# Key-value sums in 32-column strips, fewer transpose instructions for weights, and a re-ordered instruction list in a fused attention and MLP kernel

## The chip, the cores and the metric

The kernel runs on one core of a Trainium2 chip. The metric is device time in microseconds (us) from launch to end; lower is better. The engines are named as in the profile: PE (TensorE, matrix products; PEld are its weight loads), DVE (VectorE), ACT (ScalarE), POOL (GpSimd) and SP (the queue that issues most DMA transfers).

## The reference

`x` has 2048 tokens of 448 features. It is normalised once (`xn`), and two blocks read `xn`; the result is `x` plus both.

```python
x = A_x
xn = _layernorm(x, axis=-1)
return x + _A_ref(xn, ...) + _B_ref(xn, ...)

# A: 16 heads of 28 features
pq = einsum("bhsd,hdf->bhsf", q, w_phi);  pk = einsum("bhsd,hdf->bhsf", k, w_phi)
phi_q = concatenate([softmax(pq), softmax(-pq)]);  phi_k = concatenate([softmax(pk), softmax(-pk)])
kv  = einsum("bhsf,bhsd->bhfd", phi_k, v);   z = einsum("bhsf->bhf", phi_k)
num = einsum("bhqf,bhfd->bhqd", phi_q, kv);  den = einsum("bhqf,bhf->bhq", phi_q, z)
o = num / (den + 1e-6)                       # and o @ wo

# B
h = gelu(layernorm(xn) @ w1);  hs = (four column groups of h, shifted by 1, -1, 2, -2 tokens) @ w2
x1 = xn + hs;  result x1 + gelu(layernorm(x1) @ w3) @ w4
```

Here `q`, `k`, `v` are the three 448-column parts of `xn @ wqkv`.

## The kernel before

Tokens are cut into 16 tiles of 128 (`NT`). The 448 features lie as four chunks that overlap (`lap`), so that a product over 448 features is two streams of 64-row matmuls, one in the upper and one in the lower half of the array's rows, which are issued in turn and run side by side (`LO`, `HI`, `row_pairs`). The profile prints such matmuls as `64*128`, and those that use all rows as `128*128`.

`Recorder` writes every instruction into a list per engine and works out the semaphore waits from what each reads and writes; each engine then runs its list in order. So the order of the calls in the source is the order of each queue. For PE it also keeps the tile mode (rows in use): a write to a bank that was last written in another mode waits for that earlier matmul. All operations are issued from a few helper lines: L204 (matmul), L208 (PE transpose), L212 (ACT), L216 (DVE and POOL), L219 (DMA transpose), L222 (DMA).

Three parts run one after the other, with overlap.

1. The head and the chain (`chain`, a hand-written list). `spin` and `hold` (`HD`) are filler matmuls on constants. For each tile: statistics on DVE (`"m"`), root on ACT or POOL (`"q"`, `"r"`), scaling on DVE (`"a"`) or on POOL (`"p"`, which first issues a negation), then the transposition of the tile into `xnT`: by PE (`XT`: 8 transposes of 64 columns, `xn_T`, and a copy out of PSUM, `xn_out`) or by a DMA transpose on SP (`XD`, `xn_Td`). With `xnT` come the value projection (`ZV`: 7 matmuls of 448 columns), the w1 product (`ZW`, `ZH`, `ZR`), and `fold` (`FO`), which multiplies the query and the key weights by `w_phi` ahead of the tokens: the weights come transposed by DMA (`load_wT`) into `wT`, and `phi_blocks` multiplies `w_phi` by a block mask `mb`, which POOL builds from a memset and two selects, into `bd`. `rest_T` turns the last columns of `h` into `hRT`, and `h_shift` makes the shifted copies by DMA. `HF` are the halves of the first key pair (0), the first w2 pair (1) and the first query pair (2).
2. The middle, from the list under `play`: per pair of tiles the key product (`k0`, `k1`, exponentials on ACT), the query product (`q0`, `q1`), the w2 product (`w0`, `w1_`, with the sum `w2_out` on DVE), `kn` (reduction and reciprocal on DVE), `kx` (the product with the reciprocal on POOL), `lo`, `sc`, `A`, `G` (second layernorm and its transposition), and `K`, the key-value sums of one tile (`kv_tile`).
3. The end: `a`, `b` (w3 product and gelu), `N` (`num_tile`: numerators, division), `f` (w4 and wo products), `S` (stores).

`kv_tile` takes, for one tile, 16 matmuls of 59 columns: `phik` is the stationary operand and `vaug` (values, a column of ones, a column of zeros for each head) streams, over 64 tokens each, into banks 6 and 7. After the last tile `kv_copy` adds the two banks (two DVE operations), `kv_blocks` moves rows by four matmuls with `pick`, and two DVE and two ACT copies write `kvq`, which `num_tile` reads.

Of the kernel before, what the change touches and what calls it, by code (L numbers as in the profile page):

```python
# [224 lines left out]
def bass_parallel_sum__linear_kernel_hedgehog__mixer_s_mlp__prompt_kernel(  # L225
# [17 lines left out]
    with es:  # L243
# [55 lines left out]
        bd = view(g_r, D)  # L299
        wphi = view(g_r, NC * DH, at=1024).rearrange("p (c f) -> p c f", c=NC)  # L300
        kvq = new("kvq", 8 * 64).rearrange("p (b e) -> p b e", b=8)
        kvT = view(w1_r, 512)
        kvf = view(w1_r, 512, F32, at=1024)
        pick = view(w1_r, 2 * 128, at=3072).rearrange("p (s c) -> p s c", s=2)
        ident = new("ident", 128)
        maskb = new("maskb", CR)
# [73 lines left out]
        R.dma(wphi[0:CR, :, :], A_w_phi.rearrange("(c q) e f -> (q e) c f", q=4))  # L380
# [17 lines left out]
        def load_w4(eng="SP"):  # L398
# [21 lines left out]
        mb = maskb[0:CR, :].rearrange("p (h e) -> p h e", h=4)  # L420
        R.ew(pool, "memset", maskb[0:CR, :], 1.0)
        R.op(pool, lambda e: e.affine_select(mb, mb, pattern=[[-DH, 4], [0, DH]], compare_op=ALU.is_ge,
                                             fill=0.0, base=0, channel_multiplier=1), [maskb[0:CR, :]], [maskb[0:CR, :]])
        R.op(pool, lambda e: e.affine_select(mb, mb, pattern=[[DH, 4], [0, DH]], compare_op=ALU.is_ge,
                                             fill=0.0, base=DH - 1, channel_multiplier=-1),
             [maskb[0:CR, :]], [maskb[0:CR, :]])

        def phi_blocks():
            R.ew(dve, "tensor_tensor", bd[0:CR, :].rearrange("p (c h f) -> p c h f", c=NC, h=4),
                 wphi[0:CR, :, :].unsqueeze(2).to_broadcast([CR, NC, 4, DH]),  # L430
                 mb.unsqueeze(1).to_broadcast([CR, NC, 4, DH]), op=ALU.mult)

        def late_3():
            pad = phik.rearrange("p t g e -> p (t g) e")[:, :, DH:HP]
            R.op(pool, lambda e: e.memset(pad, 0.0), [pad], [xn[:, NT - 2, :]])
            R.ew(pool, "memset", kvq[:, :, :], 0.0)
            R.ew(pool, "memset", eq[:, 4:8, :, :, DH:HP].rearrange("p t s h e -> p (t s h) e"), 0.0)

        def kv_ones():
            for h in range(4):  # L440
# [53 lines left out]
        def fold(t, m, b, n):  # L494
            def side(k, hi):
                r, c0, c1 = (slice(64, CR), 2 * DH, CR) if hi else (slice(0, 64), 0, 3 * DH)
                return [(banks[b + k][:, CR * c + c0:CR * c + c1],
                         wT[r, t, c, START[m + k]:START[m + k] + 128], bd[r, CR * c + c0:CR * c + c1], n == 0 and c == 0)
                        for c in range(NC)]
# [62 lines left out]
        def chain(jobs, lag, even):  # L562
            at, upper, seen = [0, 0], deque(), {}
            odd, left = False, sum(j[0] == "zip" for j in jobs)
# [37 lines left out]
            for kind, make, then, *mid in jobs:  # L602
# [12 lines left out]
                else:  # L615
                    for n, item in enumerate(make(LO, (0, 1, 3) if odd else (0, 1, 2, 3))):
# [6 lines left out]
                    left -= 1  # L623
                    odd = not odd and left > even
# [478 lines left out]
```

## Time and profile before

| | |
|---|---|
| median of 3 runs | 171.56 us (170.79 to 171.65) |
| profiled execution: span from its first to its last instruction | 169.2 us (the page has no other time for it) |
| median less that span | 2.4 us |
| PE busy | 165.9 us (98%), 2359 matmuls recorded |
| DVE, ACT, POOL busy | 109.6, 82.1, 92.2 us |
| matmuls of the key-value sums | 256 of 59 columns |
| PE transposes of xn tiles | 112 of 64 columns |
| DMA transposes of query and key weights | 8 |

The profile gives, for groups of instructions, the busy time and the mean length of one. Matmuls are pipelined and their ends are modelled, so what a matmul takes from PE is read from one start to the next. A timeline row has the start in us, the busy time in us, the engine, the line, the operation and its tiles, and the number of instructions merged.

### The profile page before, as it was taken

Reading aid. Unit: us, or ns where it says so; the run is one execution under the profiler, and the core shown is the slowest. Engines: PE = TensorE matmul, PEld = TensorE weight load, DVE = VectorE, ACT = ScalarE, POOL = GpSimd, SP = SyncE. Lnnn points to the kernel's source line nnn. Section 1 sums busy time; section 2 is a strip of 40 time slices with the busy share of each in tenths; the row PEclk is TensorE's granted clock in tenths of the full one; section 3 lists DMA queues with packets and bytes.
Section 4 is the critical chain, followed back from the end, with each engine's and each line's share of the span. In section 5 each row is a group of like instructions: output and inputs, shape, how many; then the busy total and the mean of one; then the engine's idle time right before and its main releaser. Section 6 shows DMA issues by size and latency. Waiting matters only on the chain.

```text
span 169.2 us, 5423 instructions
## 1 busy us (share of the span) xinstructions
PE 165.9 (98%) x2359; PEld 99.3 (59%) x2359; DVE 109.6 (65%) x248; ACT 82.1 (49%) x110; POOL 92.2 (54%) x124
## 2 busy tenths in 40 slices
PE   8999999999999999999999999999999999999994
PEld 7776778667786555554554555555545555444453
DVE  3998866159999899929685896718617586220031
ACT  3599975797998878646242422024204041144000
POOL 5288980005999999951792264396730845404040
PEclk9999999999999999999999999999999999999999
DMA  5995579999599985671076664434554422310031
GB/s 162 364 197 103 98 135 293 164 330 149 99 141 183 278 97 149 86 134 27 7 118 127 95 135 55 84 73 42 135 68 93 59 61 62 83 60 4 0 109 54
DMA packets 50567, 19.93 MB, mean 118 GB/s; under 512 B 41712, under 2 KB 49840, under 8 KB 50544
## 3 DMA queue, kind: packets, MB, share of 16 engines
q1 hardware_dynamic: 49424, 18.71, 57.1%
q10 hardware_dynamic: 1120, 0.89, 1.6%
q8 instruction: 18, 0.29, 0.8%
q14 instruction: 5, 0.04, 0.1%
HBM read 7.14 MB, written 1.84 MB: 53 GB/s over the span
## 4 chain that ended last, share of the span: by engine, by line
PE 95%; DMA 1%; DVE 1%; issue 0%; DVEq 0%
PE banks L204 94%; DMA xtok<-in_A_x_dram 1%; PE banks L208 1%; DVE st L216 1%; DVE mv L216 0%; DVE xn L216 0%; DVE vaug L216 0%; DVEq L166 0%
## 5 line engine op out<-in xcount | busy, mean ns | idle before, releaser
L212 ACT ACTIVATE phik<-banks 128x1024 bf16<-128x1024 f32 (+1 forms) x44 | 42.2, 987 | 60.7 <-PE banks L204 60.5
L216 DVE TENSOR_TENSOR vaug<-banks,vaug 128x464 f32<-128x464 f32 (+3 forms) x65 | 32.8, 513 | 26.1 <-PE banks L204 24.5
L204 PE MATMUL banks<-gT,w 64*128 64x512 bf16 x392 | 48.2, 376 | 0.0
L204 PE MATMUL banks<-w,phik 64*128 64x448 bf16 (+3 forms) x434 | 45.2, 343 | 0.0
L216 POOL TENSOR_TENSOR xnT<-vaug 128x196 bf16<-128x196 f32 (+1 forms) x32 | 18.1, 587 | 29.6 <-DVE vaug L216 29.6
L204 PEld LDWEIGHTS banks<-w,phik 64*128 64x128 bf16 (+1 forms) x434 | 22.3, 94 | 20.1 <-issue 0.4
L204 PE MATMUL banks<-wv,xnT 64*128 64x448 bf16 (+2 forms) x222 | 32.9, 346 | 0.0
L723 POOL TENSOR_TENSOR phik<-phik,rks 128x1792 bf16<-128x1792 bf16 x8 | 25.6, 3219 | 8.5 <-DVE rks L216 8.5
L204 PEld LDWEIGHTS banks<-gT,w 64*128 64x128 bf16 x392 | 17.9, 94 | 18.0 <-ACT phik L212 0.4
L216 POOL TENSOR_TENSOR vaug<-xn,xtok 128x448 f32<-128x448 bf16 x16 | 16.2, 1034 | 12.7 <-DVE vaug L216 12.7
L204 PEld LDWEIGHTS banks<-wv,xnT 64*128 64x128 bf16 (+1 forms) x222 | 14.0, 94 | 7.7 <-PE banks L204 0.3
L204 PE MATMUL banks<-xnT,w 64*128 64x512 bf16 (+1 forms) x105 | 16.6, 334 | 0.0
L204 PE MATMUL banks<-wpk,xnT 64*128 64x448 bf16 x112 | 16.6, 349 | 0.0
L216 DVE TENSOR_REDUCE ksum<-phik 128x64 f32<-128x1792 bf16 x8 | 16.0, 2000 | 0.0
L204 PE MATMUL banks<-wpq,xnT 64*128 64x448 bf16 x112 | 15.7, 349 | 0.0
L212 ACT ACTIVATE hi<-banks 128x896 bf16<-128x896 f32 x16 | 13.7, 923 | 2.0 <-PE banks L204 2.0
L204 PE MATMUL banks<-w,hT 64*128 64x448 bf16 x96 | 13.6, 349 | 0.0
L216 POOL TENSOR_TENSOR rs<-mv,mhalf 128x1 f32<-128x1 f32 (+1 forms) x13 | 9.4, 727 | 6.2 <-DVE mv L216 6.0
L216 DVE RECIPROCAL vaug<-banks 128x16 f32<-128x16 f32 x16 | 4.0, 250 | 12.6 <-PE banks L204 12.6
L216 DVE TENSOR_TENSOR xn<-banks,xn 128x512 bf16<-128x512 f32 (+1 forms) x16 | 8.9, 598 | 2.3 <-PE banks L204 2.3
L216 POOL TENSOR_SCALAR g_tok<-xn,rs 128x512 bf16<-128x512 bf16 x13 | 9.9, 774 | 0.2
L216 DVE BATCH_NORM_STATS2 st<-xtok 128x6 f32<-128x448 bf16 x16 | 9.6, 601 | 0.2 <-DMA xtok<-in_A_x_dram 0.2
(67 smaller groups left out, 172.7 us busy)
## 6 DMA issues: line engine op xcount, KB each, us to landing
w<-in_B_w_dram SPq DMA_DIRECT2D x2, 896.0 KB, 5.8
out_dram<-vaug SPq DMA_DIRECT2D x15, 112.0 KB, 1.8
w<-in_B_w_dram SPq DMA_DIRECT2D x1, 1568.0 KB, 8.6
xtok<-in_A_x_dram SPq DMA_DIRECT2D x2, 448.0 KB, 6.3
wv<-in_A_wo_dram SPq DMA_DIRECT2D x2, 224.0 KB, 3.3
xtok<-in_A_x_dram SPq DMA_DIRECT2D x3, 112.0 KB, 3.6
xtok<-in_A_x_dram ACTq DMA_DIRECT2D x3, 112.0 KB, 4.2
w<-in_B_w_dram SPq DMA_DIRECT2D x1, 336.0 KB, 4.1
```

The costliest lines, as they stand in the source:

```text
L204: self.op("PE", lambda e: e.matmul(out, lhsT, rhs, start=start, stop=stop, skip_group_check=True), [out], [lhsT, rhs], tile=self._tile(lhsT))
L208: self.op("PE", lambda e: e.transpose(out, in_, ident), [out], [in_, ident], tile=self._tile(in_))
L212: self.op("ACT", lambda e: e.activation(out, in_, func, **kw), [out], [in_] + aps)
L216: self.op(eng, lambda e: getattr(e, name)(out, *args, **kw), [out], aps)
L723: R.op(pool, lambda e: e.tensor_tensor(ph, ph, wide, op=ALU.mult), [ph], [ph, wide, *after])
```

## The change

- `kv_tile` swaps the operands: `vaug` of one head (30 columns) is stationary, `phik` (64 columns: both softmax signs of the head) streams, over all 128 tokens. Four heads go to four strips of 32 output rows in bank 6. There are still 16 matmuls a tile, now of 64 columns. In the list the calls of `K` stand in three groups on PE: 6, 5 and 5 tiles.
- `kv_turn` (a DVE transpose of 128 x 256 from PSUM) and `kv_blocks` (one DVE product with a mask `pick` of two columns) replace the two-bank add, the four matmuls and the copies.
- `load_wT` transposes two chunks of 128 columns in one DMA: four instructions instead of eight, placed at other points of the chain. The chunks are 128 columns wide instead of 112, so the mask covers 128 rows by 672 columns (112 by 112 before), `phi_blocks` has two operations, and `fold` takes three or four heads at a time: 48 matmuls of 84 and 8 of 112 columns instead of 32 of 84 and 32 of 56.
- Tiles 14, 13, 12 and 8 are transposed by DMA too (`XB`), besides 10 and 11. 80 PE transposes instead of 112.
- POOL scales 13 of the first-layernorm tiles (8 before), the first two among them; six tiles of the second layernorm are scaled on DVE (three before).
- The chain, the list under `play`, the banks and the split of each product between the two row halves (a string of 0 and 1) are new. The numerators (`num_tile`) stay as they are.

The core of the diff:

```diff
-        bd = view(g_r, D)
+        bd = view(g_r, NC * 6 * DH).rearrange("p (c h f) -> p c h f", c=NC, h=6)
+        mb = view(g_r, NC * 6 * DH, at=1600).rearrange("p (c h f) -> p c h f", c=NC, h=6)
...
-        def load_wT(t, cs):
-            for c in cs:
-                e0 = t * D + CR * c
-                R.dma_t(wT[:, t, c, 0:D], A_wqkv[:, e0:e0 + 128], after=[wv] if t and not c else [])
-        load_wT(1, (0, 1, 2, 3))
-        load_wT(0, (0,))
+        def load_wT(t, c, n=2):
+            R.dma_t(wT[:, t, c:c + n, 0:D], A_wqkv[:, t * D + 128 * c:t * D + 128 * (c + n)], after=[wv])
...
-        R.ew(pool, "memset", maskb[0:CR, :], 1.0)
+        R.ew(pool, "memset", mb[:, :, :, :], 1.0)
...
         def kv_tile(i):
-            def side(k, rows):
-                return [(banks[6 + k][:, 64 * n:64 * n + VP + DH + 1],
-                         phik[rows[0]:rows[1], i, 4 * n:4 * n + 4, :].rearrange("p g e -> p (g e)"),
-                         vaug[rows[0]:rows[1], i, 2 * VP * n:2 * VP * n + VP + DH + 1]) for n in range(8)]
-            row_pairs(side(0, LO), side(1, HI), i == 0)
+            for n in range(4):
+                for j in range(4):
+                    h = 8 * (j // 2) + 2 * n + j % 2
+                    R.mm(banks[6][HP * j:HP * j + VP, 64 * n:64 * n + 64], vaug[:, i, VP * h:VP * h + VP],
+                         phik[:, i, 2 * h:2 * h + 2, :].rearrange("p g e -> p (g e)"), i == 0 and n == 0, False)
...
-        def kv_copy():
-            n61 = [a.rearrange("p (n e) -> p n e", n=8)[:, :, 0:VP + DH + 1] for a in (banks[6], banks[7], kvf, kvT)]
-            R.ew(dve, "tensor_copy", n61[2], n61[0])
-            R.ew(dve, "tensor_tensor", n61[3], n61[1], n61[2], op=ALU.add)
+        def kv_turn():
+            R.ew(dve, "transpose", kvT[:, :], banks[6][:, 0:256])
...
+            R.ew(dve, "tensor_tensor", kvq[:, :, 0:2 * VP].rearrange("p b (h e) -> p b h e", h=2)[:, :, :, 0:DH + 1],
+                 kvT.rearrange("p (b e) -> p b e", e=HP)[:, :, 0:DH + 1].unsqueeze(2).to_broadcast([128, 8, 2, DH + 1]),
+                 pick.unsqueeze(1).unsqueeze(3).to_broadcast([128, 8, 2, DH + 1]), op=ALU.mult)
...
+        def XB(i):
+            return "both", ((), ()), ((xn_Td, i),)
...
-            L(("m", 0), ("q", 0, 1)), do(load_wT, 0, (1, 2, 3)), L(("m", 1), ("q", 1, 1), ("a", 0), ("a", 1)), HD(3, 3),
-            HD(6, 3), HD(3, 3), L(("m", 2)), XT(0, 0, 1, "ACT"), L(("q", 2, 1)), HD(6, 3), L(("m", 3), ("m", 4)),
-            XT(1, 2, 1, "ACT"), L(("p", 2), ("q", 3, 1), ("q", 4, 1), ("a", 3)), HD(6, 3), HD(6, 3), ZV(0, EV(0, "ACT", 1)),
...
-            do(h_shift, 1), do(kv_picks), HF(1, 1), do(rest_T, 1)], 400, 0)
+            L(("m", 0)), L(("q", 0, 1)), HD(4, 3), HD(4, 3), L(("p", 0)), HD(0, 3), L(("m", 1)), L(("m", 2)),
+            L(("q", 1, 1)), L(("m", 3)), L(("p", 1)), L(("q", 2, 1)), XT(0, 6, 1, "ACT"), XT(1, 1, 1, "ACT"),
+            L(("p", 2)), do(load_phi), L(("m", 4)), HD(5, 3), ZV(0, EV(0, "ACT", 1)), L(("q", 3, 1)), L(("r", 4, 1)),
...
+            inside(3, ZR(0, 5, (rest_out, 0, 5), (rest_T, 0)), XT(9, 1, 1, "2")), FO(0, 0, 0), XB(10),
+            ZV(9, EV(9, "ACT", 1)), do(load_w2), do(h_shift, 0), ZR(1, 4, (rest_out, 1, 4)), FO(0, 0, 1),
+            ZV(11, EV(11, "ACT", 1)), do(kv_ones), FO(0, 2, 0), ZW(2, 2, EW(2, 2, 1)), ZW(2, 1, EW(2, 1, 1)),
+            ZW(2, 0, EW(2, 0, 1)), do(rest_T, 1), FO(0, 2, 1), ZV(10, EV(10, "ACT", 1)), HF(0, 0), do(load_w4),
+            HF(1, 0), do(late_3), HF(2, 0), do(h_shift, 1), HF(0, 1), HF(1, 1), HF(2, 1), do(load_w3, 0)], 400,
+            "101100100101011100011010010101100")
```

More of the change, by code (lines that the diff above doesn't have):

```diff
@@ L495, in side @@
             def side(k, hi):
[L496 to L499, printed above, removed]
+                r = []
+                for c, (h0, h1) in enumerate(((2, 5), (2, 6), (3, 6)) if hi else ((0, 3), (0, 3), (1, 4), (1, 4))):
+                    p = slice(64 * hi, 64 * hi + 64)
+                    r.append((banks[b + k][:, DH * (4 * c + h0):DH * (4 * c + h1)],
+                              wT[p, t, c, START[m + k]:START[m + k] + 128],
+                              bd[p, c, h0:h1, :].rearrange("p h f -> p (h f)"), n == 0 and c == 0))
+                return r
             return side(n, 0), side(1 - n, 1)
@@ L560, in v_out, with chain @@
                 R.ew(dve, "tensor_copy", vd, vs)
-        def chain(jobs, lag, even):
+        def chain(jobs, lag, heavy):
             at, upper, seen = [0, 0], deque(), {}
-            odd, left = False, sum(j[0] == "zip" for j in jobs)
+            turns = iter(heavy)
             def where(item):
@@ L744, in kv_blocks @@
[L744 to L757 removed]
+                R.ew(dve, "memset", pick[HP * q:HP * q + HP, q % 2:q % 2 + 1], 1.0)
```

148 lines of the change are left out of this document (66 added, 82 removed).

## The prediction

> **What bounds the kernel now.** I read the busy shares of the page first, then the chain in order of time, then the busy time by stage, then PE's timeline around each edit.
>
> ```profile
> span 169.2 us, 5423 instructions
> PE 165.9 (98%) x2359; PEld 99.3 (59%) x2359; DVE 109.6 (65%) x248; ACT 82.1 (49%) x110; POOL 92.2 (54%) x124
> ```
> ```profile
> 5.33 0.40 PE banks L208 x8
> ...
> 13.24 0.14 PE banks L208 x8
> ...
> 16.56 0.35 PE banks L208 x24
> ...
> 24.82 142.05 PE banks L204 x1955
> 166.87 0.02 issue
> ```
> ```profile
> 34.00:80.00 46.00, 46.00 (x702) 28.77 (x700) 39.81 (x65) 36.64 (x43) 33.53 (x20) 1.00 0.81 152
> ```
>
> From 5.33 us to 166.87 us the chain is PE alone; its last piece, 142 us long, has no other releaser in it. Between 34 and 80 us, where the key-value sums lie, PE is busy for all 46.00 us, and DVE (39.81) has little room. So the time is a head of 5.3 us, the matmuls, and a tail of 2.3 us. An edit gains what it takes off PE and loses what it adds to the head or opens as a hole. Work taken off ACT or DVE gains nothing by itself.
>
> The sum is made on the span of the profiled execution, 169.2 us; the page gives no other time for it. The median of the runs, 171.56 us, is 2.4 us above that span (the runs 1.6 to 2.5), and I carry those 2.4 over. A measurement of this kernel can tell about 0.5% (0.86 us) from no change.
>
> **Key-value sums: what they cost now.** Per token tile, 16 matmuls of 59 columns, on two 64-row halves of the array at once.
>
> ```profile
> 73.77 1.67 PE L204 MATMUL banks<-gT,w 64*128 64x512 bf16 x14
> 75.27 0.62 PE L204 MATMUL banks<-vaug,phik 64*128 64x59 bf16 x32
> 75.73 1.67 PE L204 MATMUL banks<-gT,w 64*128 64x512 bf16 x14
> 77.39 0.39 PE L204 MATMUL banks<-w 64*128 64x232 bf16 x4
> 77.60 1.68 PE L204 MATMUL banks<-gT,w 64*128 64x512 bf16 x14
> ```
>
> A row's start to the next row's start is what a group takes from PE (the printed length holds the last one's pipeline too). Two token tiles take 75.73 - 75.27 = 0.46 us, 0.23 each, 14.4 ns a matmul; one half starts one every 28.8 ns. Sixteen tiles: 3.7 us.
>
> After, there are again 16 matmuls a tile, now 128 rows by 30 output columns with 64 columns streamed, in four column strips that all write bank 6. No row shows column strips. Bounds: if the four run at once, each strip at the pace of the 64-column transposes (24 in 0.35 us on two halves, 29.2 ns a half), 7.3 ns a matmul, 0.117 us a tile, 1.9 us in all: 1.8 less. If only two starts fit in that time, 14.4 ns: nothing gained. If they queue, 28.8 ns: 7.4 us, 3.7 more. I take the first: the two halves now start within the same slot and neither slows the other, and the strips write disjoint partitions as the halves use disjoint rows.
>
> **What the new shape adds.** The sums leave the 64-row mode. Before they lay in it between other 64-row matmuls; after they stand on PE in three groups (tiles 0, 9, 3, 2, 8, 1; then 10, 5, 4, 12, 7; then 15, 13, 6, 14, 11), so six changes of mode. The trace has one such change at full speed:
>
> ```profile
> 158.78 0.92 PE L204 MATMUL banks<-w,phik 64*128 64x448 bf16 x8
> 159.54 0.73 PE L204 MATMUL banks<-wv,xnT 64*128 64x448 bf16 x6
> 160.20 2.82 PE L204 MATMUL banks<-w,phik 128*128 128x448 bf16 x14
> ```
>
> Eight take 159.54 - 158.78 = 0.76 us, 95 ns each; six more would end at 160.11, and the 128-row one starts at 160.20: 0.09 us. Six cost 0.54 us (bounds 0, if it drains under other work, and 1.1, twice that). Key-value net: -1.8 + 0.5 = -1.3 us.
>
> [...]
>
> **The turn of the sums.** Four pick matmuls go (77.60 - 77.39 = 0.21 us), and PE's wait before them: the 14 ahead start at 75.73 and, like those at 73.77 (1.50 us to the next row), would end at 77.23; 0.16 us until 77.39. The DVE transpose and multiply that replace two copies, an add and casts stand before the first numerators; 28 matmuls of 107 ns (3.0 us) lie between on PE as cover. Without it their length would be a hole. I bound that by what they replace:
>
> ```profile
> 75.93 0.65 DVE L216 COPY w<-banks 128x472 f32<-128x472 f32 x1 [3.01 <-PE banks L204]
> ...
> 78.01 0.76 DVE L216 CAST kvq<-banks 32x232 bf16<-32x232 f32 x2
> ```
>
> From 75.93 to 78.77 is 2.8 us, less than the cover. Net -0.21 - 0.16 = -0.37 us.
>
> **xn tiles by DMA.** Tiles 14, 13, 12 and 8 join 11 and 10 on the DMA path: 32 transposes of 14.6 ns go, -0.47 us, and four DMA transposes are added on SP. Four for query/key weights (two chunks each) replace eight:
>
> ```profile
> 5.74 13.09 SPq L219 DMA_TRANSPOSE hi<-in_A_wqkv_dram  x8
> 18.88 2.26 SPq L222 DMA_DIRECT2D w<-in_B_w_dram  x3
> 21.18 2.58 SPq L219 DMA_TRANSPOSE xnT<-xn  x2
> 23.80 0.96 SPq L222 DMA_DIRECT2D w<-in_B_w_dram  x1
> 24.80 3.74 SPq L222 DMA_DIRECT2D hT<-hT  x6
> 28.59 1.31 SPq L219 DMA_TRANSPOSE hRT<-gT  x1
> ```
>
> One weight transpose holds SP 1.64 us, one xn tile 1.29. If a two-chunk one costs no more, SP is freed of 6.5 us and takes on 5.2; if twice, nothing is freed and 5.2 are added. What counts is the order: w2, the six shifts and hRT now stand behind tile 10's transpose, which waits for POOL to scale tile 10. The w2 matmuls that need them began here:
>
> ```profile
> 33.36 0.35 PE L204 MATMUL banks<-w,hT 64*128 64x448 bf16 x1
> ```
>
> After, POOL scales 13 tiles, not 8. After the first at 5.9 us (below), eleven more up to tile 10 at 1.06 us and nine reciprocal roots at 0.6 end near 23 us. Then 1.3 (tile 10), 2.3 (w2), 3.7 (shifts), 1.3 (hRT): SP is through at 31.6 us, against 29.9 before. PE asks about 1.3 us earlier than 33.36, since the first half of the first query pair and the second half of the first key pair (14 matmuls of 95 ns) now follow it.
>
> ```profile
> gT<-g_tok SPq DMA_TRANSPOSE x16, 2.5
> ...
> hRT<-gT SPq DMA_TRANSPOSE x2, 4.5
> ```
>
> A landing takes 2.5 to 4.5 us from issue, so hRT, issued at 30.3, is there at 32.8 to 34.8, against a need near 32.5 (33.36 less 1.3 and 0.5 of transposes, plus 0.6 of the head and three matmuls): a hole of 0.3 to 2.3 us, or none if the shifts land sooner now that the w3 load (issued at 23.80) has gone behind them. I take 0.2.
>
> The three fold groups of heads change 64 matmuls of 84 and 56 columns into 56 of 84 and 112: about the same columns, priced at zero.
>
> **The head.** The mask is now 128 x 672 instead of 112 x 112, and POOL, not DVE, scales the first xn tile.
>
> ```profile
> 2.25 0.19 POOL L216 MEMSET maskb<- 112x112 bf16 x1
> 2.51 0.30 POOL L422 TENSOR_SCALAR_AFFINE_SELECT maskb<-maskb 112x112 bf16<-112x112 bf16 x1
> 2.88 0.30 POOL L424 TENSOR_SCALAR_AFFINE_SELECT maskb<-maskb 112x112 bf16<-112x112 bf16 x1
> 4.29 0.20 ACT L212 ACTIVATE rs<-mv 128x1 f32<-128x1 f32 x1 [2.23 <-DVE mv L216]
> 4.91 0.77 DVE L216 TENSOR_SCALAR xn<-xtok,mv,rs 128x512 bf16<-128x512 bf16 x2
> 6.07 0.78 PE L204 MATMUL banks<-const-bfloat16-1.0 64*128 64x128 bf16 x12
> 6.69 1.53 PE L204 MATMUL banks<-wv,xnT 64*128 64x448 bf16 x9
> 8.22 0.19 POOL L216 TENSOR_SCALAR rs<-mv 128x1 f32<-128x1 f32 x1 [0.39 <-ACT rs L212]
> 8.51 0.77 POOL L216 TENSOR_SCALAR xn<-xtok,rs 128x512 bf16<-128x512 bf16 x1
> ```
> ```profile
> L435 POOL MEMSET phik<- 128x2048 bf16 x1 | 1.8, 1809 | 0.0
> L216 POOL MEMSET hi<- 128x512 bf16 x2 | 1.1, 528 | 0.0
> L216 POOL TENSOR_TENSOR rs<-mv,mhalf 128x1 f32<-128x1 f32 x9 | 5.3, 598 | 0.6 <-DVE mv L216 0.4
> ```
>
> A POOL memset grows by (1809 - 528)/1536 = 0.83 ns an element: 672 take 0.66 us, +0.47. A select at that slope takes 0.77 us; if all its time grows with size, 1.8; I take 0.9, nearest to the 512-element scaling at 0.77. So POOL is free at 3.18 + 0.47 + 1.2 = 4.85 us (4.6 to 6.7), after the root at 4.49; negation and scaling take 1.06 (8.22 to 9.28): the first xn tile stands at 5.9, not 5.30, the second at 7.0, and POOL then sets the pace. The last of the early tiles, 6, comes after five scalings from there and two roots: 5.9 + 5.3 + 1.2 + 0.1 = 12.5 us. Before, its transposes were at 13.24, but after two value projections (14 x 95 ns) that now come later, so 11.9 in the new order. The head costs 0.6 us (0.4 to 2.4).
>
> **Sum.** -1.3 - 0.37 - 0.47 + 0.2 + 0.6 = -1.3 us: span 167.9, time 171.56 - 1.3 = 170.3 us. The other re-ordering I price at zero: DVE and POOL hold the same reductions and products, and PE has other matmuls to run beside them. That cover is thin where DVE has 6 us of room in 46: a w2 sum that now stands behind one more reduction holds its PSUM pair back by that much, and PE with it once the other pairs are used up.
>
> ```profile
> L216 DVE TENSOR_REDUCE ksum<-phik 128x64 f32<-128x1792 bf16 x8 | 16.0, 2000 | 0.0
> ```
>
> One such case would cost up to 2.0 us; it goes into the upper end of the range.
>
> **Rivals.**
> 1. *Strips queue, slower.* If a strip's matmul cannot start until the one before it has streamed, or its weights wait for it, the sums cost 28.8 ns each: -1.3 becomes +4.2, the time 175.8. The point of decision is 14.4 - 0.54 us/256 = 12.3 ns a matmul; above it this edit loses. For it: no strip in the trace. Against: the halves overlap. [...]
> 2. *Two at a time, no gain.* 14.4 ns stays the pace: +1.8, time 172.1.
> 3. *Full clock comes later.* Filler matmuls go at 52 ns just before 6.69 (12 in 0.62 us) and real ones at 95 ns for 448 columns, 27 ns for 128, right after: PE doubles its speed there. After, PE waits 0.6 us longer for the first tile and 1.1 us for the second, with no filler between them. If that puts the doubling off to 2.4 us after the first real matmul, half of it is lost: +1.2, time 171.5. [...]
> 4. *Late transposes.* The hole before the w2 matmuls is 2.3 us, not 0.2: time 172.4.
>
> **How the numbers follow.** Forecast 0.55, strips queue 0.12, two at a time 0.11, late clock 0.10, late transposes 0.09; 0.03 for less than all (switches free, head 0.4, no holes: 171.56 - 1.8 - 0.84 + 0.4 = 169.3). The forecast's own range, switches 0 to 1.1 and head 0.4 to 1.4, is 169.4 to 171.7; the range 168.9 to 173.4 takes in all but queued strips. Faster by over 0.5% (below 170.7): most of the forecast and the 0.03, 0.53. Within 0.5%: the rest of it, the late clock, half of two at a time, a quarter of late transposes, 0.23. Slower (above 172.4): 0.24.
>
> **What would show it.** Right: 96 strip matmuls in about 0.7 us, a step of 0.1 us at each end of a group, the first xn transposes near 5.9 us, no idle row on PE after 13 us. Wrong: groups of 2.8 us, a PE wait for hRT or for a late xnT near 20 to 33 us, 52 ns fillers after 8 us.

## The result, and the profile after

| | before | after |
|---|---|---|
| median | 171.56 us (170.79 to 171.96, 7 runs) | 174.38 us (173.84 to 176.57, 7 runs) |
| ratio after to before | | 1.0169, 95% interval 1.0142 to 1.0197 |
| span of the profiled execution | 169.2 us | 174.8 us |

The change makes the kernel slower by 1.7%. The forecast was 170.3 us, range 168.9 to 173.4: wrong in sign and in range. The ratios, here and below, leave out executions in a slow state, the profiled one of after among them (176.57 us; the other six took 173.84 to 174.62), so its profile overstates the loss by some 2 us. The same sources of loss, in other sizes, stand in the profile of `e0_after` below.

The page of after, busy times and slices:

```profile
span 174.8 us, 5334 instructions
...
PE 166.2 (95%) x2315; PEld 94.0 (54%) x2315; DVE 107.0 (61%) x239; ACT 80.6 (46%) x109; POOL 96.6 (55%) x131
...
PE   8599999999999779999999999999999999999994
...
PEclk9979999999999999999999999999999999999999
```

PE's sum has hardly moved (165.9 to 166.2), but it no longer fills the span. PE's busy share dips in the second slice (4.4 to 8.7 us) and in the fourteenth and fifteenth (57 to 66 us); the mean granted clock is 0.90 in the second and 0.71 in the third (8.7 to 13.1 us). The view of PE's waits names them (engine and line, what it waited for: us in total, times, longest). Before:

```profile
PE banks L204 <- PEq L1088: 0.8, 1, 0.8
```

After:

```profile
PE banks L204 <- ACT hi L212: 2.9, 3, 1.2
PE banks L208 <- POOL xn L216: 2.3, 3, 1.0
PE banks L204 <- PEq L1083: 0.8, 1, 0.8
PE banks L204 <- issue: 0.3, 1, 0.3
```

Before, PE waited only for its own start. After, it waits 2.9 us for the query exponentials (`hi` holds them) and 2.3 us for xn tiles that POOL scales.

**The head**, PE's timeline of after:

```profile
5.97 0.29 PE L208 MATMUL banks<-ident,xn 64*128 64x64 bf16 x8 [1.01 <-POOL xn L216]
7.09 0.29 PE L208 MATMUL banks<-ident,xn 64*128 64x64 bf16 x8 [0.82 <-POOL xn L216]
...
7.51 0.94 PE L204 MATMUL banks<-wv,xnT 64*128 64x448 bf16 x3
...
8.48 1.68 PE L204 MATMUL banks<-wv,xnT 64*128 64x448 bf16 x7
```

The first tile comes at 5.97 us and the second at 7.09, as forecast (5.9 and 7.0). The value matmuls start at 7.51 (6.69 before). But seven of them from 8.48 on take 1.68 us, while the same seven take 0.92 in `e11_fill` below: PE is at half rate again (granted clock 0.50 in the second row below). Busy times by stretch (length, then PE, PEld, DVE, ACT, POOL, granted clock, DMA share, GB/s), the stretches cut at the changes of the clock in the trace:

```profile
4.48:7.90 3.42, 1.59 (x41) 1.01 (x35) 2.60 (x8) 1.44 (x5) 3.12 (x7) 1.00 1.09 362
7.90:11.31 3.41, 3.41 (x41) 2.43 (x41) 2.76 (x12) 1.19 (x4) 2.86 (x8) 0.50 1.20 323
```

The full clock was granted at 4.48, went back to half at 7.90 after 3.42 us in which PE was busy for 1.59, and returned at 11.31 for good (1.00 from there to the end). In the kernel before it stayed from 6.68 us on (1.00). 3.41 busy us at half rate are 1.7 us lost.

**The middle**, timelines of after (SP, ACT, PE in turn):

```profile
40.07 1.11 SPq L222 DMA_DIRECT2D w<-in_B_w_dram  x2
41.56 18.52 SPq L219 DMA_TRANSPOSE eqT_lo<-hi  x7
```
```profile
55.93 1.73 ACT L212 ACTIVATE hi<-banks 128x896 bf16<-128x896 f32 x2 [1.99 <-DMA eqT_lo<-hi]
...
60.80 1.73 ACT L212 ACTIVATE hi<-banks 128x896 bf16<-128x896 f32 x2 [1.53 <-DMA eqT_lo<-hi]
```
```profile
57.71 0.74 PE L204 MATMUL banks<-w,hT 64*128 64x448 bf16 x6 [1.00 <-ACT hi L212]
...
62.59 0.74 PE L204 MATMUL banks<-w,hT 64*128 64x448 bf16 x6 [1.19 <-ACT hi L212]
...
68.55 0.95 PE L204 MATMUL banks<-phik,vaug 128*30 128x64 bf16 x96
70.20 3.20 PE L204 MATMUL banks<-gT,w 64*128 64x512 bf16 x28 [0.69 <-ACT hi L212]
```

Read from the bottom: PE waits for a PSUM pair that ACT has yet to empty into `hi`; ACT waits because `hi` has room for eight tiles and the query transposes (`T`, the seven DMA transposes in the SP row) have not yet read the old ones; those stand on SP right behind two loads of w3 of 896 KB each. The DMA view from 12 to 44 us gives the median from issue to landing, first of before, then of after:

```profile
eqT_lo<-hi SPq DMA_TRANSPOSE x2, 3.2
```
```profile
eqT_lo<-hi SPq DMA_TRANSPOSE x2, 12.2
```

### The profile page after: what moved, and what is told of

Same layout as the page of the kernel before. It is cut to its first block, busy times and chain, and to the rows that moved or that the text cites. A ratio compares the mean times of both kernels' runs of the same rounds, so it can differ in the third digit from the quotient of the medians.

```text
span 174.8 us, 5334 instructions
## 1 busy us (share of the span) xinstructions
PE 166.2 (95%) x2315; PEld 94.0 (54%) x2315; DVE 107.0 (61%) x239; ACT 80.6 (46%) x109; POOL 96.6 (55%) x131
## 4 chain that ended last, share of the span: by engine, by line
PE 83%; POOL 5%; ACT 3%; SPq 3%; DMA 2%; DVE 1%; issue 1%; POOLq 0%; ACTq 0%
PE banks L204 82%; SPq L219 3%; POOL xn L216 2%; DMA eqT_lo<-hi 2%; ACT phik L212 2%; POOL rs L216 1%; ACT hi L212 1%; PE banks L208 1%; DVE st L216 1%; POOL g_tok L418 1%; POOL g_tok L420 1%; POOL g_tok L216 0%; POOL hi L216 0%; DVE mv L216 0%; DVE vaug L216 0%
## 5 line engine op out<-in xcount | busy, mean ns | idle before, releaser
L212 ACT ACTIVATE phik<-banks 128x1024 bf16<-128x1024 f32 (+1 forms) x44 | 41.2, 987 | 63.9 <-PE banks L204 63.8
L204 PE MATMUL banks<-gT,w 64*128 64x512 bf16 x392 | 46.9, 376 | 0.7 <-ACT hi L212 0.7
L204 PE MATMUL banks<-wv,xnT 64*128 64x448 bf16 (+2 forms) x222 | 35.0, 355 | 0.0
L204 PEld LDWEIGHTS banks<-gT,w 64*128 64x128 bf16 x392 | 18.5, 94 | 20.1 <-ACT hi L212 0.8
L204 PE MATMUL banks<-xnT,w 64*128 64x512 bf16 (+1 forms) x105 | 17.3, 338 | 0.0
L204 PE MATMUL banks<-w,hT 64*128 64x448 bf16 x96 | 13.0, 349 | 2.2 <-ACT hi L212 2.2
L204 PE MATMUL banks<-wpk,xnT 64*128 64x448 bf16 x112 | 14.9, 349 | 0.0
L204 PE MATMUL banks<-wpq,xnT 64*128 64x448 bf16 x112 | 13.7, 349 | 0.0
L216 POOL TENSOR_SCALAR xn<-xtok,rs 128x512 bf16<-128x512 bf16 x13 | 10.4, 799 | 1.3
```

The lines of the kernel that those rows point to most:

```text
L204: self.op("PE", lambda e: e.matmul(out, lhsT, rhs, start=start, stop=stop, skip_group_check=True), [out], [lhsT, rhs], tile=self._tile(lhsT))
L212: self.op("ACT", lambda e: e.activation(out, in_, func, **kw), [out], [in_] + aps)
L216: self.op(eng, lambda e: getattr(e, name)(out, *args, **kw), [out], aps)
```

## The experiments

Three theories. **Queue**: the w3 loads ahead of the query transposes, with the order of these, are the loss. **Head**: the late first tiles and the clock that falls back are. **Strips**: the column strips gain less than their rows say. The letters in the expectations are those of the run that they were written for.

| kernel | median us | before, same chip | ratio, 95% interval |
|---|---|---|---|
| e5_strips | 171.42 | 171.20 | 1.0010 (0.9981 to 1.0038) |
| e6_strips4 | 171.55 | 171.20 | 1.0014 (0.9981 to 1.0046) |
| e1_w3_later | 176.84 | 171.20 | 1.0249 (1.0130 to 1.0368) |
| e2_mask_later | 176.56 | 171.20 | 1.0303 (1.0204 to 1.0402) |
| e0_after (the changed kernel again) | 176.51 | 171.45 | 1.0253 (1.0172 to 1.0333) |
| e7_w3_early | 174.88 | 171.45 | 1.0201 (1.0170 to 1.0232) |
| e8_w3_early_T | 176.18 | 171.45 | 1.0258 (1.0207 to 1.0310) |
| e9_first | 175.36 | 171.45 | 1.0246 (1.0207 to 1.0284) |
| e10_second | 171.66 | 171.62 | 1.0015 (0.9987 to 1.0043) |
| e11_fill | 173.82 | 171.62 | 1.0131 (1.0090 to 1.0172) |
| e13_dve_head | 175.31 | 171.62 | 1.0213 (1.0160 to 1.0266) |
| e14_all | 175.18 | 171.62 | 1.0213 (1.0161 to 1.0265) |
| e15_fill_w3 | 175.00 | 171.04 | 1.0195 (1.0154 to 1.0236) |
| e16_head_all | 173.64 | 171.04 | 1.0142 (1.0118 to 1.0165) |
| e17_second2 | 172.29 | 171.04 | 1.0079 (1.0052 to 1.0105) |
| e19_no_fill | 174.87 | 171.04 | 1.0211 (1.0187 to 1.0236) |
| e20_fill_queue | 176.37 | 170.99 | 1.0271 (1.0218 to 1.0325) |
| e18_second3 | 170.19 | 170.99 | 0.9950 (0.9919 to 0.9982) |

### The strips alone

`e5_strips`: the kernel before with `kv_tile`, `kv_turn`, `kv_blocks` and `pick` of after; the calls of `K` stay where they were, scattered.

> The kernel before, with one part of the change alone: the sums in four column strips of bank 6, the DVE transpose and the masked product in place of the add, the four pick matmuls and the copies. The tiles stay scattered as they were. Theory D (strips run four at once at 7.3 ns a matmul, each entry and each exit of the mode costs about 0.1 us): the sums take 1.9 us and not 3.7, 13 separate places cost 26 x 0.1 = 2.6, the turn saves 0.4: 0.4 us slower, 171.5 to 172.4. Rival (changes of mode are hidden where PE has other work): 169.4.

`e6_strips4`: the same, with the calls of `K` gathered in four places.

```diff
-(K, 0), ... (K, 4), ... (K, 2), ... (K, 6),
+(K, 0), (K, 4), (K, 2), (K, 3), (K, 1), (K, 7), (K, 5), (K, 6),
```

> As the strips alone in the kernel before, but with the tiles of the sums brought together in four groups (8, 2, 2, 4). Theory D: 8 changes of mode at 0.1 us and not 26, so -1.8 + 0.8 - 0.4 = -1.4 us against the kernel before: 169.8 to 170.4, and 1.5 to 2 us under the scattered strips. Rival (grouping puts a hole before the group, or the mode costs nothing): no better than the scattered strips.

171.42 and 171.55 against 171.20: no difference that can be measured. The strips are not the loss. By the trace the scattered strips of `e5_strips` stand in 10 groups, not 13. That gathering them gained nothing as yet is taken up with `e18_second3`; in `e6_strips4` PE waits 0.5 us for a load of weights, a new wait.

### The queue, first attempt, and the mask

`e1_w3_later`: the two w3 loads move behind the sixth and the seventh query transpose.

```diff
-HF(2, 1), do(load_w3, 0)], 400,
+HF(2, 1)], 400,
...
-(load_w3, 1), (k0, 2), (kn, 0),
+(k0, 2), (kn, 0),
...
-(T, 3), (w1_, 6),
+(T, 3), (load_w3, 0), (w1_, 6),
...
-(T, 4), (A, 2),
+(T, 4), (load_w3, 1), (A, 2),
```

> The changed kernel, with its two w3 loads (0.9 MB each) moved in SP's queue from ahead of the query transposes to behind the sixth and the seventh of them. Theory A (the w3 loads delay the query transposes; the exponentials of later query tiles wait for the transposes because they write the same eight-tile buffer; PE waits for the exponentials): the two PE waits of 1.35 and 1.54 us at 56 to 62 us and the 0.9 us after the first group of sums go, and the time falls by 2.5 to 3.5 us, to 171 to 172. Theory B (the transposes are late because of their own order and because ACT is late): the waits stay within 0.5 us and the time stays at 174 to 174.5.

176.84 us, no gain. The waits for `hi` fell from 2.9 to 0.9 us, and another took their place: the gate transposes, now queued behind the loads, come late.

```profile
PE banks L208 <- POOL xn L216: 2.3, 3, 1.1
PE banks L204 <- DMA gT<-g_tok: 1.8, 1, 1.8
PE banks L204 <- ACT hi L212: 0.9, 2, 0.6
```

`e2_mask_later`: POOL builds the mask (a memset and two selects) after the root of tile 14, not at the start.

```diff
-        R.ew(pool, "memset", mb[:, :, :, :], 1.0)
...
-L(("r", 14, 1)), do(load_wT, 1, 0),
+L(("r", 14, 1)), do(mask), do(load_wT, 1, 0),
```

> The changed kernel, with POOL's memset and two selects of the 128 x 672 mask moved from the start to behind the scaling of the early tiles (still ahead of the fold). Theory C (the head waits for POOL's mask): the first xn transposes start near 5.4 us and not 5.97, the second set near 6.5 and not 7.1, and the time falls by 0.5 to 0.7 us, or by up to 2 us where the full clock is then held. Rival (x and the statistics set the head, the mask is hidden): first transposes stay at 5.9 and the time stays within 0.2 us of the changed kernel's 174.4.

176.56 us, slower. The first xn transposes came at 5.46 instead of 5.97 us. But the third tile was loaded late (its statistics begin at 7.35 us), and PE waits 2.1 us for the copies of the first two, which stand behind that tile's root on ACT (see `e13_dve_head`). A later wait on POOL grew from 0.4 to 1.5 us, behind the mask that now stands at 16 us, and the half clock lasted from 7.98 to 14.8 us. So this run moved the first tile and does not say what the mask's place alone is worth.

### Which half of the order

`e0_after` is the changed kernel again, `e7_w3_early` and `e8_w3_early_T` have both w3 loads at 13 us, where the DMA engines were less than half busy (share 0.48 from 13.1 to 17.5 us in after), and the second also the query transposes in the order of the tiles.

```diff
+do(load_wT, 1, 2), do(load_w3, 0), do(load_w3, 1), ZV(7,
...
+(T, 2), (T, 3), (k0, 3), (q1, 2), (T, 4), (T, 5), ... (A, 1), (T, 6), (T, 7), (AD, 0)
```

> The changed kernel once more, unaltered, on the chip of the three kernels below, so that they have their own yardstick. Expected: 173.8 to 174.7 us. If the half-rate stretch of the clock after the head, seen from 7.9 to 11.3 us in the first profile, belongs to the slowest executions alone, a profile at 172 to 173 us of span has less PE time in it; the two waits of PE for the query exponentials at 56 to 63 us (1.35 and 1.54 us) should stand in every execution, since they come from the order of the queue.

> Changed kernel, but both loads of w3 (1.8 MB) are issued in the first stage, behind the key-weight transposes at about 13 us, where the DMA engines are mostly idle, not right ahead of the first query transpose. Theory A, the loads saturate the DMA engines from 38 to 50 us and hold the first query transposes for 12 us: these land in 3 to 5 us, the two waits at 56 to 63 us (2.5 us) close, but the last pair of query exponentials still waits for the eighth query transpose, which stands in SP's order behind three gate transposes; 171.6 to 173.0 us. Theory B, the loss lies in the first stage (mask, clock, POOL's scalings): no change, 173.8 to 174.7. Theory C, w3 merely moves the stall to whatever transfer comes next, as it did when it was moved later: 173.5 to 175.

> As the kernel with both w3 loads early, and the query transposes in the order of the tiles, 0 to 7, with the eighth ahead of the first three gate transposes. Theory A: no exponential waits for a transpose any longer, PE has no gap over 0.5 us between 35 and 85 us, and 0.5 to 1.5 us go beyond the kernel with the early loads alone: 171.0 to 172.0. Theory B: 173.5 to 174.5.

`e0_after` took 176.51 us, not the 173.8 to 174.7 expected, and its profile has one wait for `hi`, not two or three:

```profile
PE banks L204 <- ACT hi L212: 1.5, 1, 1.5
```

It runs at half rate until about 13.5 us (a value matmul's row is 0.57 us long at 12.91 and 0.35 at 13.65), so PE is 1.4 us later there than in the profile of after (the same transposes start at 13.77 and at 12.39), and waits 1.4 us less for `hi` (1.5 for 2.9); the spans are 174.9 and 174.8 us. The two losses therefore do not simply add up. Why the medians of the same kernel, 174.38 and 176.51, differ was not found.

`e7_w3_early` has no wait for `hi` left on PE and stays 2.0% above the kernel before. Its gain must be read at a like clock: its profiled execution, like that of `e0_after`, runs at half rate until about 13.5 us (rows of 0.57 us at 12.91, 0.35 at 13.60), and there the spans are 173.4 and 174.9 us, the medians 174.88 and 176.51. So the queue is real, worth 1.5 to 1.6 us at that clock, as much as the wait that went, and not the whole. By times alone this would not be shown: one execution of `e0_after` took 174.03, and against the first measurement of after (174.38) nothing is gained. `e8_w3_early_T` gained nothing more: 1.1 us of waiting for xn tiles that come by DMA stand in it, and the half clock until 14.1 us.

`e9_first` joins the first stage of after (first half of w3 early) to the second of before; `e10_second` the first stage of before to the second of after.

> The changed kernel's first stage (mask, weight and xn transposes by DMA, its order) with the second stage in the order of the kernel before (column strips scattered as the tiles come, first half of w3 loaded early, second half behind seven query transposes). It prices the first stage alone; the kernel before with scattered strips took 171.42. Theory A, the second stage's order holds the loss: 171.2 to 172.4. Theory B, the first stage holds it: 173.5 or more.

> The first stage of the kernel before with the second stage of the changed one: its order of query and gate transposes, its strips in three groups; the first half of w3 loaded early as in the kernel before, the second half right ahead of the first query transpose. The complement of the kernel that took the changed first stage alone (175.36). If the first stage holds the loss: 170.5 to 171.8, with at most one wait for a query exponential left. If both stages cost on their own: 172.5 to 174.

175.36 and 171.66. The loss goes with the first stage; the second stage as such costs nothing. In `e10_second` one half of w3 still stands ahead of the query transposes and no exponential waits: in that place it takes both halves, which only the new first stage puts there. In `e9_first` 0.7 us are a wait for a bank (PE for the first key exponentials, at 40 us), which I put down to joining the two, and 1.1 us are a stop of PE at 31.2 us with no releaser (see `e19_no_fill`).

### The clock

`e11_fill`: the changed kernel with 36 more filler matmuls where PE was idle, and nothing else.

```diff
-XT(0, 6, 1, "ACT"), XT(1, 1, 1, "ACT"),
+HD(3, 9), XT(0, 6, 1, "ACT"), HD(3, 9), XT(1, 1, 1, "ACT"),
```

> The changed kernel with 36 more filler matmuls on TensorE in the head, 18 ahead of the first and 18 ahead of the second set of xn transposes, where it stands idle from 4.95 to 5.97 and from 6.13 to 7.09 us; nothing else differs, and POOL's scalings come no earlier. Theory D, the clock falls back or is granted late because a window of 3.4 us has these two idle pieces in it (full rate for good only at 11.3 to 14.1 us in five profiles with this first stage, at 6.1 to 6.7 in three with the first stage of before): full rate stays from 8.3 us or earlier, and the time falls by 1 to 2.5 us against the changed kernel: 172.3 to 174.0. Theory E, the lateness of the first tiles and POOL's later scalings themselves are what costs, the clock follows: no gain, 174 to 176.5 (two fillers at half rate take 0.11 us, so 36 of them may add 0.2 us).

173.82 us: 0.6 under the first measurement of after (174.38; the ratios' intervals overlap), 2.7 under `e0_after` (176.51, on another chip). Its PE timeline:

```profile
5.97 0.29 PE L208 MATMUL banks<-ident,xn 64*128 64x64 bf16 x8 [0.39 <-POOL xn L216]
6.10 0.69 PE L204 MATMUL banks<-const-bfloat16-1.0 64*128 64x128 bf16 x18
7.09 0.29 PE L208 MATMUL banks<-ident,xn 64*128 64x64 bf16 x8 [0.30 <-POOL xn L216]
...
8.22 0.92 PE L204 MATMUL banks<-wv,xnT 64*128 64x448 bf16 x7
```

The tiles come at the same 5.97 and 7.09, but the seven value matmuls take 0.92 us instead of 1.68: fillers that compute nothing bought full rate here. What that is worth in time these two differences bound only roughly. 2.3 us of waits for `hi` remain in it.

`e13_dve_head` lets VectorE scale tiles 0 and 1 as before; `e14_all` adds the early w3 and the ordered transposes.

```diff
-L(("p", 0)), ... L(("p", 1)),
+L(("m", 1)), L(("q", 1, 1), ("a", 0), ("a", 1)),
```

> The changed kernel with tiles 0 and 1 scaled by VectorE behind their statistics, as in the kernel before, not by POOL behind the mask; the mask stays where it is. First xn transposes at 5.3 and 5.9 us instead of 5.97 and 7.09. Theory D and theory E both: the first tile of values some 0.8 us earlier, full clock from about 6.7 us as before, together 2 to 4 us: 171.0 to 173.0; what is left over 171.4 is the second stage's waits (1 to 2.5 us of query transposes). Theory A, the second stage's order is what costs: under 1 us of gain, 173.5 or more.

> The same head by VectorE, and both w3 loads early, and the query transposes in the order of the tiles. If head and second-stage order are the two causes and nothing else is: 169.8 to 171.3, at or under the kernel before, since the strips in three groups and 32 PE transposes less are then left as gains (about 1.3 us by the changed kernel's rows). If another cause stays in the first stage (POOL's scaling of tile 15, the folds' weights, 0.8 and 0.5 us of PE waiting): 171.5 to 172.8.

175.31 and 175.18: both expectations missed. The first tile is there at 5.46, but PE goes on only at 7.34:

```profile
6.06 0.22 PE L204 MATMUL banks<-const-bfloat16-1.0 64*128 64x128 bf16 x1
7.34 0.50 PE L204 MATMUL banks<-const-bfloat16-1.0 64*128 64x128 bf16 x5 [1.07 <-ACT xnT L212]
```
```profile
6.60 0.20 ACT L212 ACTIVATE rs<-mv 128x1 f32<-128x1 f32 x1 [1.25 <-DVE mv L216]
6.71 1.07 ACT L212 ACTIVATE xnT<-banks 128x512 bf16<-128x512 bf16 x2
```

In ACT's list the root of tile 2, which waits for that tile's statistics on DVE (done at 6.57 us), stands ahead of the copies of tiles 0 and 1 (in the kernel before it stands behind the first). So two items set the start of the value matmuls at 7.5 us, the scaling on POOL and this root; taking one away left the other, the idle PE, and the half clock (until 13.9 us).

`e19_no_fill` is the converse: the kernel before without the 36 fillers of its head.

```diff
-HD(3, 3), HD(6, 3), HD(3, 3), ... HD(6, 3), ... HD(6, 3), HD(6, 3),
```

> The kernel before without the 36 fillers of its head, nothing else changed: the converse of the filler kernel. Theory D, idle pieces of TensorE in a window of 3.4 us hold the clock at half rate in the next: full rate for good only at 8 to 14 us instead of 6.1 to 6.7, 172.3 to 174.5. Theory E, the clock is not set by them: 170.8 to 171.8, as the fillers do no work.

174.87 us, 3.8 slower. The clock went full at 3.85, back to half at 7.27, full at 10.68, though real work began earlier than before (values at 6.17 us). By the rows this costs 1.1 us: the first matmuls for `hRT` start at 25.60 instead of 24.48. The rest is one gap:

```profile
28.94 0.28 PE L204 MATMUL banks<-w,xnT 64*128 64x64 bf16 x4
32.00 0.19 PE L204 MATMUL banks<-w,xnT 64*128 64x64 bf16 x1 [2.74 <-issue]
```

The profile names no releaser. In the trace a 16 KB block of an instruction queue starts to arrive at 29.12 us and takes 1.33, so it is in 1.55 us before PE goes on. In after, `e0_after` and `e9_first` PE also stands still between two matmuls of one kind at 31.0 to 32.4 us, for 0.32, 0.66 and 1.10 us with no releaser, and goes on 1.4 to 1.6 us after such a block is in. That PE had run out of instructions fits; no run tested it. So this run shows the clock go back where the fillers are left out (PE busy for 1.85 us of the 3.42 ahead of it), and by its time alone it would overstate what they are worth.

### Both together

`e15_fill_w3` is `e8_w3_early_T` with the fillers. `e16_head_all` has the VectorE scaling of tiles 0, 1 and 15, tile 2's root behind the copy of tile 0, 16 more fillers (by the trace, 82 for 66; the expectation says 22), one half of w3 early and one behind the query transposes. `e20_fill_queue` is `e11_fill` with the queue alone mended: the first half of w3 where w4 was, the second behind eight ordered query transposes, w4 behind the third gate transpose.

> The kernel with both w3 loads early and the query transposes in order (176.18) plus the 36 fillers of the filler kernel (173.82, with 2.8 us of waiting for query exponentials at 54.6 and 59.4 us left in it). If the clock of the head and the queue of the query transposes are two independent causes, both go: 171.0 to 172.4. If the late clock only covers for the transposes, or the early w3 loads cost elsewhere (they stood beside gaps of 0.9 and 0.7 us at 24 to 26 us): 173 to 174.

> The changed kernel with its first stage's starts taken back: tiles 0 and 1 scaled by VectorE, the root of tile 2 on ScalarE behind its copy of tile 0 instead of ahead of it, 22 more fillers (2 to 3 pairs at each of the idle places), tile 15 scaled by VectorE; first half of w3 early, the second behind the query transposes, these in order. If the idle pieces of the head (with the clock) and the queue are the whole loss: 170.0 to 171.5, values start at 6.7 us as before and full clock by 6.8. If the clock is still late, a third cause sets it: 173 or more.

> The changed kernel with the 36 fillers in the head (173.82 alone, with 2.8 us of waits for query exponentials left) and with no large load ahead of the query transposes: the first half of w3 goes where w4 went (34 us), the second behind the eighth query transpose, w4 (not used before 80 us) behind the third gate transpose; the query transposes in the order of the tiles. Nothing is loaded ahead of the xn transposes, which the two kernels with both halves of w3 at 13 us showed to wait 6.4 to 6.6 us for them. If the clock of the head and the queue are two causes that add up: 170.8 to 171.9, about the kernel before. If another transfer is merely held in turn (the gate transposes behind w4): 172.3 to 173.5.

175.00, 173.64 and 176.37: each missed its lower expectation, the first and the last the upper one too. In `e15_fill_w3` the clock is full from 6.59 us and no exponential waits, but the early loads hold the xn transposes (chain of waits):

```profile
18.63 6.55 DMA xnT<-xn
```

and PE waits 2.6 us for them. In `e16_head_all` the clock is full from 6.22 us and values start at 6.78, but tile 2 (0.7 us) and tile 15 (0.7 us) are scaled late. `e20_fill_queue` is the most telling one. Up to 64.6 us PE waits for no transfer; then the load of w4 (1568 KB), issued right ahead of the fourth gate transpose, holds that for 7.9 us:

```profile
63.83 0.95 PE L204 MATMUL banks<-phik,vaug 128*30 128x64 bf16 x96
67.97 4.88 PE L204 MATMUL banks<-gT,w 64*128 64x512 bf16 x28 [3.18 <-DMA gT<-g_tok]
72.67 0.74 PE L204 MATMUL banks<-w,hT 64*128 64x448 bf16 x6
```
```profile
68.00:71.40 3.40, 3.40 (x18) 1.35 (x20) 3.33 (x5) 0.00 (x0) 3.40 (x3) 0.50 0.50 111
```

The wait cost 3.2 us, and the half clock behind it 1.7 more: these 28 matmuls take 4.70 us from start to start, 3.02 in `e18_second3` below. Taking both off the span leaves 174.2 - 3.2 - 1.7 = 169.3 us, the span of before (169.2). That is worked out from rows; no kernel with the changed first stage was measured at it.

### The second stage on the old first stage

`e17_second2` and `e18_second3` are `e10_second`, whose one large gap (PE waits 1.2 us at 36.3 us for the first w2 sum to leave its bank) came from joining the stages, with the first steps of the second stage in another order. The diff is that of `e18_second3`; `e17_second2` also moved `(load_w3, 1)` behind `(T, 6)`, between query transposes.

```diff
-(load_w3, 1), (k0, 2), (kn, 0), (k0, 1), (w0, 2), (k1, 1), (lo, 1), (T, 0), (kx, 0), (w1_, 2),
+(load_w3, 1), (w0, 2), (kn, 0), (k0, 1), (w1_, 2), (k1, 1), (k0, 2), (lo, 1), (T, 0), (kx, 0),
```

> The kernel before's first stage with the changed second stage (171.66, with one gap of 1.60 us at 35.9 us where the first key matmuls of the second stage wait for a bank that the first stage still uses), its first six steps put in the order of the kernel before, and the second half of w3 behind seven query transposes. If that gap is an artefact of joining the two and nothing else waits: 170.0 to 170.8, faster than before by the strips in three groups. If another wait takes its place: 171.2 to 171.8.

> The kernel before's first stage with the changed second stage, the second half of w3 at its head as in the kernel that took 171.66 (there no exponential waited for a query transpose), and only the first key and w2 matmuls in another order, so that none waits for the bank of the first w2 sum (the 1.60 us gap at 35.9 us). The kernel that moved that load between two query transposes took 172.29 with a wait of 2.2 us. If the strips in three groups gain what their rows say (about 1.2 us on the sums and 0.4 on the turn, less the mode changes): 170.1 to 170.8, under the kernel before. If a wait takes the place of the gap: 171.2 to 171.8.

`e17_second2`: 172.29, slower than before by 0.8%. Its chain of waits shows the queue once more (L222 issues the second half of w3, 896 KB; the query transpose behind it takes 5.96 us):

```profile
50.04 0.59 SPq L222
50.63 0.05 issue
50.68 5.96 DMA eqT_lo<-hi
```

`e18_second3`: 170.19 against 170.99, ratio 0.9950 (0.9919 to 0.9982). It beats the kernel before by 0.5%, clear of its interval, and with it the changed one. Its only PE wait is the start:

```profile
PE banks L204 <- PEq L1077: 0.8, 1, 0.8
```

## Why the prediction was wrong

**Right: the strips.** The rivals "strips queue" (28.8 ns a matmul) and "two at a time" (14.4) fell. Two groups in after:

```profile
77.67 0.94 PE L204 MATMUL banks<-phik,vaug 128*30 128x64 bf16 x80
78.55 3.19 PE L204 MATMUL banks<-gT,w 64*128 64x512 bf16 x28
81.67 0.82 PE L204 MATMUL banks<-phik,vaug 128*30 128x64 bf16 x80
82.43 1.04 PE L204 MATMUL banks<-gT,w 64*128 64x512 bf16 x8
```

80 strip matmuls take 82.43 - 81.67 = 0.76 us with the step out of the mode, 9.5 ns each; at the 7.3 ns of the forecast they are 0.58, so that the step out and a slower pace cost 0.18. The step in lies ahead of the row: the 28 matmuls from 78.55 would end at 81.57 (3.02 us, as in `e18_second3`), 0.10 us before it. So this step cost about the 0.09 forecast. The size of the gain was too large: key-value sums and turn were put at -1.7 us, and `e18_second3`, which has them and no new wait, gained 0.8, the rest of its new order included. Its groups take 1.05 us (96 matmuls), 0.75 and 0.91 (80 each) from their start to the next matmul, 2.71 in all; with three steps in of 0.10 that is 3.0 us against 3.7 before, a gain of 0.7 where 1.3 was forecast. In `e5_strips`, with ten groups and so twenty steps, nothing was left.

**Right: the first tiles, and hRT.** 5.97 and 7.09 us against 5.9 and 7.0; no PE row of after waits for hRT, and rival 4 fell. With hRT there was luck: its transposes were issued at 32.27 and 33.96 us, not by 30.3, and were in time because PE, late from the head, asked at 35.77. In `e16_head_all`, where values start at 6.78 us, PE waits 0.3 us for hRT.

**Wrong: the price of the head.** "The head costs 0.6 us (0.4 to 2.4)" counted the delay of the tiles and not the clock behind an idle PE (busy for 1.59 us of 3.42 in after, then half clock for 3.41). Rival 3 named the clock, at 1.2 us and a chance of 0.10, but as a release that comes later; no run shows its 2.4 us from the first real matmul to the doubling. In fact a clock already granted was taken back (after: full for good only 3.8 us behind the first value matmul, 11.31 for 7.51), or PE kept half rate until about 13.5 us (`e7_w3_early`). The late tiles themselves cost 0.8 us at the first value matmul (7.51 for 6.69); the half clock 1.7 us in the profile of after; tile 15, scaled by POOL at 18.9 us, 0.4 us of PE waiting: 2.9 us in that execution. The part on the early tiles also looked for POOL alone; the ACT root ahead of the copies was as late (`e13_dve_head`).

**Wrong: "The other re-ordering I price at zero."** This step failed, and its reason with it: "PE has other matmuls to run beside them". PE runs its list in order and `hi` holds eight tiles, so a late query transpose stops ACT and then PE. I followed SP up to hRT and stopped there; the w3 loads, moved from 23.80 and 52.06 us to 40.07, stand in the same timeline one row above the query transposes. Cost: 2.9 us of PE waits in the profile of after, 1.5 in that of `e0_after`; 1.6 us by time at a like clock (`e7_w3_early` against `e0_after`).

**The sum.** Forecast -1.3 us on the span, measured +5.6 in the profiled execution. PE's new waits (2.9 + 2.3 + 0.3 us) and its longer busy time (166.2 for 165.9) account for it. That busy time holds the 1.7 us of half clock, so everything else on PE, the fillers of the head included, takes some 1.4 us less; what the change gained there is at most that. The 0.3 us is the stop at 31.0 us, which the prediction does not have and no run explains. And no kernel with the changed first stage got back to the time of before, so that head and queue are the whole loss rests on these rows.

## What to carry to other kernels

Where a head is re-ordered, look at the idle time of TensorE and not only at when work starts: here 1.59 busy us of 3.42 stood ahead of 3.41 us at half clock (after), and fillers in the gaps kept full rate and left the first tiles at 5.97 and 7.09 us (`e11_fill`). Where a load of a megabyte is moved on a queue, list the small transfers behind it up to the next one that an engine waits for: in four kernels here a transpose behind such loads landed 6 to 12 us after its issue instead of 3 (last section), so I would put it where nothing urgent follows. And where a change is two orders in one, exchanging the halves tells more than mending suspects one by one: `e9_first` and `e10_second` placed the loss that the seven runs ahead of them had circled.

## What the runs showed of the hardware

**The clock was taken back without a long pause.** In after the two whole stretches between changes of the clock lasted 3.41 us each (4.48 to 7.90, 7.90 to 11.31). The table counts pieces of that length on or back from a change of the clock that the trace records, with the PE time in them (views of busy time by stretch):

| kernel, window | PE busy, us of 3.41 | clock in it | clock after it |
|---|---|---|---|
| e2_mask_later 4.56 to 7.98 | 1.06 | full | half |
| after 4.48 to 7.90 | 1.59 | full | half |
| e14_all 4.70 to 8.12 | 1.83 | full | half |
| e19_no_fill 3.85 to 7.27 | 1.85 | full | half |
| e19_no_fill 27.75 to 31.16 | 1.51 | full | full |
| e15_fill_w3 23.65 to 27.06 | 2.06 | full | full |
| after 59.09 to 62.51 | 2.31 | full | full |
| e16_head_all 6.22 to 9.63 | 2.51 | full | full |
| e2_mask_later 7.98 to 11.39 | 2.40 | half | half |
| e13_dve_head 7.08 to 10.49 | 3.15 | half | half |
| e13_dve_head 0.25 to 3.66 | 2.84 | half | full |
| before 3.27 to 6.68 | 3.33 | half | full |

In the last two rows, half is read from the fillers' pace (before: one every 107 ns), since the trace's first record of the clock is at the end of the window. In the heads of this table, full was lost in windows with at most 54% of PE time and kept in one with 74% (`e16_head_all`); in after, `e14_all` and `e19_no_fill` the longest single pause in such a window was about 1.1 us. But neither busy time nor the length of a pause alone orders these rows: in `e19_no_fill` a later window with 44% and a pause of 1.9 us kept full, and `e13_dve_head` left half after 2.84 us and not after 3.15. What sets the clock stays open.

**A transpose behind a large load.** From issue to landing, 12.2 us behind 1.8 MB (after), 6.0 behind 0.9 MB (`e17_second2`), 6.6 behind 1.8 MB (an xn tile, `e15_fill_w3`), 7.9 behind 1.6 MB (`e20_fill_queue`), against 3.2 for the first two query transposes of before, which have no large load right ahead. **Column strips** overlap: by the single starts in the trace of after, 16 matmuls of 64 columns, one token tile, took 116 to 134 ns from the start of one tile to the next (7.3 to 8.4 ns a matmul; 253 ns once), where a half took 29.2 ns for 64 columns in before, four times 7.3; over whole groups it was one every 8.0 (96 matmuls), 9.5 and 7.9 ns (80 each).
